# A split first exp, a moved half quarter, a moved exp and a warm-up of short matmuls in a fused convolution and feed-forward kernel

## The chip, the cores and the metric

The kernel runs on one NeuronCore of a Trainium2 chip. The metric is the device time of one execution in microseconds. TensorE (PE in the profile) multiplies, VectorE (DVE) and ScalarE (ACT) do elementwise work, GpSimd (POOL) makes masks and issues some of the DMAs, SyncE (SP) issues the others. "PEld" is TensorE loading weights, which it can do while it multiplies.

## The reference

A dynamic convolution over the last seven rows, with weights from a softmax, and behind it a feed-forward layer with a squared relu:

```python
w = weight_gen - np.max(weight_gen, axis=-1, keepdims=True)      # (8, 4096, 8 heads, 7 taps)
w = np.exp(w)
w = w / (np.sum(w, axis=-1, keepdims=True) + 1e-09)
x_pad = np.concatenate([np.zeros((B, 6, D)), x], axis=1)          # x: (8, 4096, 192)
x_unf = x_pad[:, np.arange(S)[:, None] + np.arange(7)[None, :], :].reshape(B, S, 7, 8, 24)
y = np.einsum('bshk,bskhg->bshg', w, x_unf).reshape(32768, 192)
h = np.maximum(y @ w_in, 0.0)                                     # w_in: (192, 2048)
out = h * h @ w_out                                               # w_out: (2048, 192)
```

## The kernel before

**Blocks.** The 32768 tokens go through in blocks: `BLOCKS` has two of 512 tokens and then 31 of 1024. Blocks are numbered from 0 in the code; the text calls block 0 "block one". For each block:

- *Softmax.* A `Softmax` object holds 8, 16 or 32 rows of tokens per partition (`FIRST = 8` for the first ones, which cover 1024 tokens) and 6 rows of overlap. `load` fetches `weight_gen`, `exp(lo, hi)` runs on ScalarE (L238), `total` sums on VectorE (L245), `recip` takes reciprocals (L252) and `scale` multiplies into `v_first` or `v_big` (L260), by four operations for each 8 rows.
- *Rows and bands.* The scaled weights are brought to one row of tokens per partition (`wr`), by DMAs through `move_rows` and `wr_load`, and for the first block by TensorE: `select_rows` multiplies with a selection matrix `sel` (L372), eight matmuls for each of five tiles, and `copy_rows` copies from PSUM (L381). `st_band` then spreads `wr` with a mask into a band matrix `bd` on VectorE (L395).
- *Convolution.* `st_conv` multiplies `x` with the bands on TensorE (L455, L527, L493), and copies the result to `y`, in the blocks that matter here on ScalarE (L467, L538).
- *Units.* `st_unit` computes one unit of the hidden layer into a PSUM tile `h` of two banks, from a ring of three that the convolution shares. In the first two blocks `first_unit` does it (L557) with two full-array matmuls ("both") and a pair of half-array matmuls that run side by side ("upper"); even units do "both" first and "upper" last, odd units the other way round. In all later blocks a unit is six half-array matmuls (L572). A relu on ScalarE (L586) follows, and a square on VectorE (L590) into `g`. The first two blocks have 8 units, the others 16.
- *Second matmul.* `quarters` is a generator; each step of it, a half quarter, is `st_mm2` (L621) over half of the hidden layer for 256 tokens, 16 full-array matmuls in the first two blocks, 32 half-array ones afterwards. It accumulates in the PSUM tiles `o0` and `o1`. Every second step for a quarter ends in `o_sum`: a copy on ScalarE (L635) and, in the later blocks, a sum on VectorE (L637), then for every second quarter a store. The steps lag behind the units.

**Order.** The order is written out by hand. `plans` gives one string for each of the first four blocks: `u` is a unit, `M` the next half quarter, `C` the next block's convolution, `E3` the next piece of exp of softmax part 3, `S3` its sums, reciprocal and scale, `B4` the bands of sub-block 4, `L5` a load of part 5 on SyncE, `P` the selection of the last rows of block two. Later blocks follow a steady string. Each engine works in program order.

**The start.** Before the first real work TensorE runs `spin(21)`: 21 matmuls of 512 columns on a zeroed tile `warm` into `wp`, which shares a PSUM bank with `o0` (L687). Meanwhile the first weights and `x` arrive, and ScalarE and VectorE do the first softmax: `s0.exp`, `s0.total`, `s0.recip`, `s0.scale`. Then come `select_rows(0, ...)`, the copies, the bands, and `st_conv_first(0, ...)`.

Of the kernel before, what the change touches and what calls it, by code (L numbers as in the profile page):

```python
# [9 lines left out]
def kernel(  # L10
# [26 lines left out]
    nc = tc.nc  # L37
# [13 lines left out]
    P = 128  # L51
# [47 lines left out]
    FIRST = 8  # L99
# [8 lines left out]
    def row_select():  # L108

        nc.gpsimd.affine_select(  # L110
            out=sel, in_=sel, pattern=[[-1, NSEL]], compare_op=AluOp.not_equal,
            fill=1.0, base=FIRST - 1, channel_multiplier=FIRST,
        )
# [543 lines left out]
    with nc.allow_low_precision("fp16 matmul pipeline"), tc.manual_schedule():  # L657
# [18 lines left out]
        warm = const.tile([P, TB], f16, name="warm")  # L676
# [3 lines left out]
        for v in v_first:  # L680
            nc.vector.memset(v, 0.0)

        wp = ps_o.tile([P, TB], f32, name="wp", tag="o0")

        def spin(n):
            for i in range(n):
                nc.tensor.matmul(out=wp, lhsT=warm[:, 0:P], rhs=warm, start=True, stop=True)  # L687

        s0, s1, s2 = parts[:3]
        spin(21)  # L690
        row_select()
        band_mask()
        s0.load(nc.sync)
# [3 lines left out]
        load_w_in(w_i[:, 1, 0], 1, nc.gpsimd)  # L697
        x_load(1)
        s1.load(nc.gpsimd)
        s0.exp(0, s0.rh)  # L700
        s0.total(0, s0.rh)
        s0.recip(0, s0.rh)
        s0.scale(0, s0.rh, nc.vector)
        x_cast(0, nc.scalar.copy, 0, 1)
# [24 lines left out]
        for q in range(4):  # L729
# [9 lines left out]
        steady_spread = "MuMuuu" * 2 + "MuCMuuu" + "MuMuuu"  # L739
        plans = {  # L740
            0: "u P B1 u u u E1 C S1 u u M u u",
            1: "L3 u u B2 M E2 B3 u M E2 u u S2 S2 u M u C u M",
            2: "L4 u u u E3 M u u u M B4 u u u u M B5 S3 u u u u M u C E3 u",
            3: "L5 L6 u u u M S3 u u u M u M E4 u u B6 u M u M B7 u u u E4 M u M C S4 u",
        }


# [49 lines left out]
        for j in range(len(plans), NBLK):  # L797
            plan, u = [], 0
# [59 lines left out]
        for j in range(NBLK):  # L858
# [5 lines left out]
            u = 0  # L864
# [76 lines left out]
```

The softmax here doesn't subtract the row's maximum and nothing guards it: scores larger than these inputs give would overflow.

## Time and profile before

| | us |
|---|---|
| median of 4 runs | 731.7 |
| lowest, highest | 731.32, 732.82 |
| profiled execution | 731.76 |
| its span, first to last instruction | 730.1 |
| TensorE busy in the span | 724.9 (99%) |
| VectorE, ScalarE busy | 626.7 (86%), 612.2 (84%) |

Rows of the timeline read: start in us, duration in us, engine, line, operation, output and input tiles with shapes, count; in brackets the idle time of the engine just before and what ended it. Rows of one kind that follow closely are merged, the duration then reaching from the first start to the last end. A matmul's end is modelled, so the distance between starts says more than a duration. Rows of the chain read: start, duration, engine, tile, line, count.

### The profile page before, as it was taken

The page shows a single profiled execution, that of the slowest core. Times are in us where ns is not written, and L with a number is a line of the kernel's source. Part 1 is how long each engine was busy: PE and PEld are TensorE (multiplying, and loading weights), DVE is VectorE, ACT ScalarE, POOL GpSimd, SP SyncE. Part 2 cuts the span into 40 slices and gives each one's busy share as a digit, 9 for nine tenths or more (in the row PEclk, how much of TensorE's full clock was granted, in tenths as well). Part 3 has the DMA queues.
Part 4 walks back from the last instruction along what each step waited for, and adds up shares of the span by engine and source line. Part 5 has one row for each costly group of instructions (what it writes and reads, how often), then busy time and mean ns, then how long its engine had stood idle before and what let it go on. Part 6 is the DMA issues. An engine that isn't in the chain of part 4 may idle for free.

```text
span 730.1 us, 30988 instructions
## 1 busy us (share of the span) xinstructions
PE 724.9 (99%) x14053; PEld 531.2 (73%) x14053; DVE 626.7 (86%) x836; ACT 612.2 (84%) x733; POOL 99.8 (14%) x145
## 2 busy tenths in 40 slices
PE   9999999999999999999999999999999999999998
PEld 4657888777777777777777777777777777777777
DVE  7998998998898988888988888988889988778753
ACT  5999888888888888888888888888888888888883
POOL 8131223321001100011000010010000110001000
PEclk9999999999999999999999999999999999999999
DMA  9555455685345442455442554343544325444012
GB/s 208 112 106 114 82 102 99 132 149 130 86 66 137 90 92 59 82 117 124 76 67 58 136 104 88 56 79 114 107 84 86 57 52 118 66 87 78 30 45 68
DMA packets 125984, 68.30 MB, mean 94 GB/s; under 512 B 85321, under 2 KB 122140, under 8 KB 125340
## 3 DMA queue, kind: packets, MB, share of 16 engines
q0 software_dynamic: 46192, 19.43, 22.6%
q1 hardware_dynamic: 79516, 46.79, 22.3%
q8 instruction: 110, 1.80, 1.0%
q14 instruction: 22, 0.18, 0.1%
q10 hardware_dynamic: 144, 0.10, 0.0%
HBM read 50.18 MB, written 28.70 MB: 108 GB/s over the span
## 4 chain that ended last, share of the span: by engine, by line
PE 99%; ACT 1%; issue 0%; DVE 0%
PE o L621 47%; PE h L572 44%; PE yp L493 4%; PE h L557 2%; PE yp L527 1%; PE wp L687 1%; PE yp L455 0%; ACT y L538 0%; PE pr L372 0%; ACT t L586 0%; ACT wr L381 0%; ACT w_i L721 0%; ACT y L467 0%; ACT xt L336 0%; ACT o_sb L635 0%
## 5 line engine op out<-in xcount | busy, mean ns | idle before, releaser
L586 ACT ACTIVATE t<-h 128x1024 f16<-128x1024 f32 x512 | 496.4, 1026 | 60.6 <-PE h L572 59.1
L621 PEld LDWEIGHTS <-g 64*128 64x128 f16 (+1 forms) x8032 | 345.2, 94 | 54.3 <-issue 2.5
L621 PE MATMUL o<-w_o,g 64*128 64x192 f16 (+1 forms) x8032 | 380.7, 243 | 0.2 <-issue 0.2
L590 DVE TENSOR_TENSOR g<-t 128x2048 f16<-128x2048 f16 (+1 forms) x287 | 307.3, 1105 | 30.0 <-ACT t L586 29.9
L572 PE MATMUL h<-y,w_p 64*128 64x512 f16 x2400 | 291.8, 376 | 0.0
L572 PEld LDWEIGHTS <-w_p 64*128 64x128 f16 x2400 | 114.1, 94 | 94.6
L395 DVE TENSOR_TENSOR bd<-wr,mask 128x4160 f16<-128x4160 f16 (+4 forms) x90 | 149.6, 1686 | 1.1 <-ACT wr L381 0.8
L637 DVE TENSOR_TENSOR o_sb<-o,o_sb 128x384 f32<-128x384 f32 x123 | 68.4, 556 | 61.2 <-ACT o_sb L635 60.3
L321 POOL DMA_DIRECT2D xt<-in_x_dram x63 | 52.7, 839 | 415.6 <-PE yp L493 362.5
L635 ACT COPY o_sb<-o 128x384 f32<-128x384 f32 x129 | 61.6, 477 | 45.7 <-PE o L621 45.2
L572 PE MATMUL h<-y,w_i 64*128 64x512 f16 x576 | 71.0, 377 | 0.3 <-ACT t L586 0.3
L572 PEld LDWEIGHTS <-w_i 64*128 64x128 f16 x576 | 32.6, 94 | 20.3 <-issue 1.6
L493 PEld LDWEIGHTS <-xt 128*32 128x32 f16 x2000 | 24.6, 95 | 10.6 <-issue 10.6
L260 DVE TENSOR_TENSOR v_big<-ex,rcp 128x112 f16<-128x112 f32 (+5 forms) x180 | 29.8, 236 | 2.0 <-DMA vd<-v_big 1.0
L503 DVE CAST y<-yp 128x1024 f16<-128x1024 f32 x25 | 30.4, 1218 | 0.0
L493 PE MATMUL yp<-bd,xt 128*32 128x104 f16 (+1 forms) x2000 | 28.4, 210 | 0.0
L238 ACT ACTIVATE ex<-wg 128x560 f32<-128x560 f32 (+4 forms) x38 | 25.9, 682 | 1.7 <-DMA wg<-in_weight_gen_dram 1.7
L245 DVE TENSOR_REDUCE ssum<-ex 128x80 f32<-128x560 f32 (+4 forms) x38 | 25.3, 666 | 1.2 <-ACT ex L238 1.2
L503 ACT CAST y<-yp 128x1024 f16<-128x1024 f32 x25 | 25.2, 1007 | 0.0
L252 DVE RECIPROCAL rcp<-ssum 128x80 f32<-128x80 f32 (+4 forms) x38 | 22.8, 600 | 1.3
L311 POOL DMA_DIRECT2D xt<-in_x_dram x7 | 3.9, 555 | 120.8 <-PE yp L493 109.4
L355 POOL DMA_DIRECT2D wr<-v_first x24 | 13.0, 562 | 24.8 <-DVE v_first L260 13.7
(41 smaller groups left out, 116.1 us busy)
## 6 DMA issues: line engine op xcount, KB each, us to landing
out_dram<-o_sb SPq DMA_DIRECT2D x63, 384.0 KB
xt<-in_x_dram POOLq DMA_DIRECT2D x42, 240.0 KB, 4.8
wg<-in_weight_gen_dram SPq DMA_DIRECT2D x4, 1064.0 KB
xt<-in_x_dram POOLq DMA_DIRECT2D x21, 192.0 KB, 4.8
wr<-vd SPq DMA_DIRECT2D x38, 80.0 KB
vd<-v_big SPq DMA_DIRECT2D x5, 512.0 KB
y<-y SPq DMA_DIRECT2D x100, 24.0 KB
wg<-in_weight_gen_dram SPq DMA_DIRECT2D x3, 616.0 KB
```

What stands on the lines that cost most here:

```text
L238: nc.scalar.activation(out=self.ex[:, lo:hi].rearrange("p r g k e -> p (r g) k e"), in_=self.wg[:, lo:hi].rearrange("p r (g e) k -> p (r g ...
L260: eng.tensor_tensor(out=bass.AP(tensor=v.tensor, offset=v.offset + lo * H * SL + lo % SL * 2 + g * SL * 2, ap=[list(v.ap[0]), [H * SL + 2, ...
L321: eng.dma_start(out=dst[:, first:last], in_=ap)
L395: nc.vector.tensor_tensor(out=bd_t[j][:, H * lo : H * (lo + len(tiles) * n)].rearrange("p (g m c) -> p g m c", g=shape[1], c=2 * SL), in0= ...
L493: nc.tensor.matmul(out=yp[p0 : p0 + 32, k - k0, a:b], lhsT=x_t[s][:, i, c0 : c0 + 32], rhs=bd[:, head // 2, e, 0 : b - a], start=True, sto ...
L503: copy(out=y[:, k0 : k0 + 2], in_=yp)
L572: nc.tensor.matmul(out=h[:, half], lhsT=w_in_chunk(w, u, slot, half), rhs=y_t[j][r0 : r0 + RT, k], start=(slot == 0), stop=(slot == NK - 1 ...
L586: nc.scalar.activation(out=t1[:, e], in_=h, func=ActF.Relu)
L590: nc.vector.tensor_tensor(out=g[:, a : e + 1], in0=t1[:, a : e + 1], in1=t1[:, a : e + 1], op=AluOp.mult)
L621: nc.tensor.matmul(out=oo[:, cc * Dm : (cc + 1) * Dm], lhsT=g[r0 : r0 + n, cc * P : (cc + 1) * P], rhs=w_o[r0 : r0 + n, fc, :], start=(fc ...
L635: nc.scalar.copy(out=o_sb, in_=o[0][:, c])
L637: nc.vector.tensor_tensor(out=o_sb, in0=o[1][:, c], in1=o_sb, op=AluOp.add)
```

## The change

Three edits in the program's order of work, none in what is computed.

- The warm-up runs 46 matmuls of 196 columns instead of 21 of 512.
- The first softmax's exp and sums run in two pieces, rows 0 to 7 and rows 8 to 13; reciprocal and scale stay whole.
- In block two (`plans[1]`) the second `M` stands behind one more unit. In block three (`plans[2]`) the second piece of `E3` leaves the end of the plan, and stands in block four (`plans[3]`) behind two units.

```diff
+        WARM = 196
         wp = ps_o.tile([P, TB], f32, name="wp", tag="o0")
 
         def spin(n):
             for i in range(n):
-                nc.tensor.matmul(out=wp, lhsT=warm[:, 0:P], rhs=warm, start=True, stop=True)
+                nc.tensor.matmul(
+                    out=wp[:, 0:WARM], lhsT=warm[:, 0:P], rhs=warm[:, 0:WARM],
+                    start=True, stop=True,
+                )
 
         s0, s1, s2 = parts[:3]
-        spin(21)
+        spin(46)
...
-        s0.exp(0, s0.rh)
-        s0.total(0, s0.rh)
+        for lo, hi in ((0, FIRST), (FIRST, s0.rh)):
+            s0.exp(lo, hi)
+            s0.total(lo, hi)
         s0.recip(0, s0.rh)
...
-            1: "L3 u u B2 M E2 B3 u M E2 u u S2 S2 u M u C u M",
-            2: "L4 u u u E3 M u u u M B4 u u u u M B5 S3 u u u u M u C E3 u",
-            3: "L5 L6 u u u M S3 u u u M u M E4 u u B6 u M u M B7 u u u E4 M u M C S4 u",
+            1: "L3 u u B2 M E2 B3 u u M E2 u S2 S2 u M u C u M",
+            2: "L4 u u u E3 M u u u M B4 u u u u M B5 S3 u u u u M u C u",
+            3: "L5 L6 u u E3 u M S3 u u u M u M E4 u u B6 u M u M B7 u u u E4 M u M C S4 u",
```

## The prediction

> **What bounds the kernel now.** I read the page first: shares of busy time, then the chain that ended last.
>
> ```profile
> span 730.1 us, 30988 instructions
> PE 724.9 (99%) x14053; PEld 531.2 (73%) x14053; DVE 626.7 (86%) x836; ACT 612.2 (84%) x733; POOL 99.8 (14%) x145
> PE 99%; ACT 1%; issue 0%; DVE 0%
> ```
>
> TensorE is the chain almost from end to end, so time is won only where it waits or works badly. The change touches the first 60 us; a microsecond that TensorE gains there reaches the end only if no other engine takes over behind it. The second view is the timeline of the first 12 us.
>
> ```profile
> 1.26 7.14 PE L687 MATMUL wp<-warm 128*128 128x512 f16 x21 [1.26 <-DVE warm L678]
> ...
> 3.84 0.94 ACT L238 ACTIVATE ex<-wg 128x784 f32<-128x784 f32 x1 [1.75 <-DMA wg<-in_weight_gen_dram]
> ...
> 4.81 0.97 DVE L245 TENSOR_REDUCE ssum<-ex 128x112 f32<-128x784 f32 x1 [1.17 <-ACT ex L238]
> ...
> 5.81 0.85 DVE L252 RECIPROCAL rcp<-ssum 128x112 f32<-128x112 f32 x1
> ...
> 6.30 1.61 PEld L687 LDWEIGHTS <-warm 128*128 128x128 f16 x8 [0.21 <-issue]
> 6.70 1.46 DVE L260 TENSOR_TENSOR v_first<-ex,rcp 128x112 f16<-128x112 f32 x8
> ...
> 8.24 1.33 PE L372 MATMUL pr<-v_first,sel 128*128 128x64 f16 x40
> ```
>
> Two things end at nearly one time. The softmax (exp, sums, reciprocal, scale) is done at 6.70 + 1.46 = 8.16. The warm-up matmuls are issued 0.427 us apart until about 6.25 (their weight loads stand at 5.51, 5.93, then 6.30) and 0.215 apart afterwards: TensorE's rate doubles there. (The granted clock reads 1.00 throughout; it does not show this step, the spacing does.) The last one's columns end at 8.24, and there the row selection starts. The third view is the chain in order of time.
>
> ```profile
> 23.26 1.32 PE o L621 x16
> 24.58 0.75 PE h L557 x4
> 25.34 1.43 PE o L621 x16
> 26.76 2.37 PE h L557 x12
> ...
> 51.74 1.50 ACT y L538 x2
> 53.24 0.31 issue
> 53.54 1.03 ACT t L586
> 54.58 0.04 issue
> 54.62 0.82 PE h L572 x6
> ```
>
> The second matmul's sixteen (L621) cost 1.32 in one place, 1.43 in another. From 51.74 to 54.62 the chain leaves TensorE for ScalarE: two copies of `y`, a piece of exp (the 0.31 of "issue": the exp stands at 53.13), then a relu.
>
> **Part 1, the start: exp and sums in two pieces, short warm-up.** ScalarE: the exp of 784 holds the engine 0.84 (the next cast starts at 4.68). Later rows have the two sizes: 448 takes 0.62 and the next starts 0.52 after, 336 takes 0.52 and holds 0.41. So the pieces end at 3.84 + 0.62 = 4.46 and 4.36 + 0.52 = 4.88, against 4.78: 0.09 of extra ScalarE time, ahead of a cast whose successor waits for its DMA until 6.18 anyway. VectorE: the sums take 0.61 (64 wide) and 0.50 (48 wide); the first starts at 4.49, the second behind it at about 5.02 and ends at 5.52, against 5.78. Reciprocal and scale are unchanged, so they end 0.26 earlier: scale at 7.90, seen by TensorE at about 7.94 (0.05 for the hand-over, as from the memset's end at 1.21 to 1.26).
>
> Warm-up: 0.427 / 512 columns is 0.834 ns each, so 196 columns take 0.163 before the step. A weight load takes 0.15 there and fits behind the matmul before it, just. After the step, sixteen L621 matmuls of 192 columns, each with its own load of 128, take 1.32, 0.0825 each; 196 columns 0.084. By 6.25 (6.25 - 1.26) / 0.163 = 30.5 are through, the other 15.5 take 1.30: the end is at 7.55 instead of 8.24. If the loads did not hide, each would cost 0.31 and 0.18 and the end would be near 11.8. The first bound is taken, for the L621 rows stream at their column count with the same loads.
>
> TensorE's own order says that the first two selection matmuls need the first half of the scale, the third its last operation. The third now starts at 8.24 + 2 x 0.03 = 8.30; it will at 7.94. Gain 0.36. It takes both edits: the split alone leaves the warm-up end at 8.24, the short warm-up alone leaves the scale at 8.16 + 0.05 = 8.21 (gain 0.09). What follows is a chain of small copies on ScalarE (8.67 to 12.6) that moves as one. Its other inputs must be there: `x_st` landed by 6.18, the mask is done at 6.27, GpSimd reads `w_st` at 9.82 and ScalarE only at 11.23, the first `w_o` loads are issued from 10.08 with 5.4 to 6.3 to landing and needed at 18.77. Nothing is late, so 0.36; from nothing (an input I take for landed is not) to 0.36.
>
> The Trainium skill (TensorE: Matmul & The Clock Gate, "Back-to-back issue gap") speaks against short matmuls: it gives about 81 ns for a stream of 128-column matmuls with loads, where the columns alone would take 56. An estimate by that, 25 ns more for each of the last 15.5, ends the warm-up at 7.93 and changes nothing.
>
> **Part 2, block two: the half quarter goes behind one more unit.** An even unit of `first_unit` ends on the pair of half-array matmuls, an odd one on the full-array pair. A unit is three streams of 0.2157 (0.647) plus one change between the two kinds: 0.75 says 0.10 for a change. The half quarter after odd unit 1 costs 1.32, the one after even unit 2 costs 1.43, and the three units behind it 2.37 = 3 x 0.647 + 4 x 0.107, the fourth change being the one on return. Moved behind unit 3 both changes at its edges go: 2 x 0.107 = 0.21. It issues 16 matmuls and one ScalarE copy of `o` (0.48), no store. The copy and the second exp piece now stand behind unit 3's relu instead of ahead of it; the bank is wanted again 8 us later, that exp's sum only at 34.03. The cover that could fail is VectorE: the last band for the next convolution ends at 30.92, the convolution starts at 31.13 and needs that band some 0.2 later. Arriving 0.21 earlier uses that up and no more: 0 to 0.06 lost, I take 0.
>
> **Part 3, blocks three and four: the exp goes behind two units.** ScalarE holds 0.41 for it at 53.13. Without it the relu of the last unit starts at 53.13 and ends at 54.15, and the third unit of block four, which waits for that relu's bank, starts at 54.21 instead of 54.62. But ScalarE has the same work until the copy of `o`:
>
> ```profile
> 57.16 0.53 ACT L635 COPY o_sb<-o 128x384 f32<-128x384 f32 x1
> ...
> 57.72 0.56 DVE L637 TENSOR_TENSOR o_sb<-o,o_sb 128x384 f32<-128x384 f32 x1
> ...
> 58.52 1.50 PE L621 MATMUL o<-w_o,g 64*128 64x192 f16 x32
> ```
>
> With the exp ahead of the third relu, copy and sum still end at 57.69 and 58.28, and the next half quarter, which writes the same two banks, cannot start before about 58.33. So 0.41 is won at 54.6 and 58.52 - 58.33 = 0.19 stays. Bounds: nothing, and the whole loss there, 3.15 from 52.11 to 55.26 for four units of 0.647, 0.56. On SyncE the load of a later weight block, which reuses that exp's input, now waits until about 56.3 (issued at 53.68 before). Queued behind it are row loads that need VectorE's scale of 59.9 anyway, and the weights are not used before block five: free.
>
> **The sum.** 0.36 + 0.21 + 0.19 = 0.76. The profiled execution took 731.76 (span 730.1 and 1.66 around it), the median is 731.7: 731.76 - 0.76 = **731.0**. Nothing after 62 us is touched, and the chain there is TensorE without a wait over 0.22.
>
> **Rivals.**
> *Larger gain.* The step of the rate stands at 6.25 in one execution; nothing fixes it there. For each microsecond that it comes later the old warm-up ends 0.5 later, the new one too, but with 0.39 to spare: up to about 0.4 more. With the whole 0.56 of part 3 that is 0.36 + 0.4 + 0.21 + 0.56 = 1.53: 730.2. For it: the runs before reach 732.82. Against: the profiled run is not faster than the median.
> *The start does not move,* because an input lands later than I read (`w_st` at 11.23 is the candidate), and part 3 is swallowed: 0.21 alone, 731.5.
> *Slower: the rate falls back.* The warm-up ends 0.69 sooner, a gap of up to 0.39 opens, and then come 4.4 us of thin selection and convolution work. If TensorE's rate halved there, it would need what it needed at first, 4.99 us of dense work, to rise, and lose half of it: 731.0 + 2.5 = 733.5. It decides where the first units after 12.3 show 0.43 instead of 0.216 between full matmuls. Against: the same thin stretch was survived before.
>
> The same page (Part 1, "What's actually happening") has the clock raised after one busy window of about 3.4 us that runs free of the kernel's start. By that the step would come between 4.7 and 8.1 and the mean gain of part 1 would be some 0.1 more, 730.9; one trace cannot show it.
>
> **How the numbers follow.** The sum 0.50, the larger gain 0.24, the start that does not move 0.18, the fall-back 0.08. About 0.2% (1.46 us) is what a measurement of this kernel can tell from no change: faster means under 730.24, slower over 733.16. The larger gain lies about that line, and most of it counts as faster: 0.22 with a little of the sum's tail; the fall-back gives slower 0.07; the rest is 0.71. Range 730.1 to 731.9: down to the larger gain, up past the second rival by the spread of the runs; the fall-back and the tails stay out.
>
> **What would show it.** Warm-up matmuls 0.163 then 0.084 apart, the last ending near 7.55; two sums at 4.49 and 5.02, the scale ending near 7.9, the selection's third matmul at 7.94. In block two 1.32 for each half quarter and units without the 0.11 beside them. The third unit of block four 0.41 nearer to its convolution, the half quarter after it held by the sum on VectorE. I am wrong if the first units of block one do not start 0.36 earlier (12.3 instead of 12.65), or if the gain at 62 us is not the gain at the end.

## The result and the profile after

The changed kernel takes 730.95 us (median of 41 runs, 730.36 to 731.73), the kernel before 731.83 (59 runs, 731.28 to 732.82). The ratio is 0.9987, 95% interval 0.9983 to 0.9992: 0.13% faster, inside the 0.2% that the prediction called no change. The forecast was 731.0.

The page of the changed kernel, the same three lines as before:

```profile
span 729.1 us, 31040 instructions
PE 723.2 (99%) x14078; PEld 531.3 (73%) x14078; DVE 626.6 (86%) x837; ACT 612.3 (84%) x734; POOL 100.2 (14%) x145
PE 98%; ACT 0%; DVE 0%; DMA 0%; issue 0%
```

The span is 1.0 shorter. TensorE fell from 99% to 98% of the chain, and ScalarE from 1% to 0%: the start is no longer a run of warm-up matmuls, and the detour over ScalarE in block four is gone. The start in the timeline:

```profile
1.26 5.43 PE L688 MATMUL wp<-warm 128*128 128x196 f16 x46 [1.26 <-DVE warm L678]
...
3.94 1.02 ACT L238 ACTIVATE ex<-wg 128x448 f32<-128x448 f32 x2 [1.85 <-DMA wg<-in_weight_gen_dram]
4.59 1.03 DVE L245 TENSOR_REDUCE ssum<-ex 128x64 f32<-128x448 f32 x2 [0.95 <-ACT ex L238]
...
6.54 1.46 DVE L260 TENSOR_TENSOR v_first<-ex,rcp 128x112 f16<-128x112 f32 x8
...
7.43 0.22 PE L372 MATMUL pr<-v_first,sel 128*128 128x64 f16 x2 [0.74 <-DVE v_first L260]
...
8.06 1.27 PE L372 MATMUL pr<-v_first,sel 128*128 128x64 f16 x38 [0.41 <-DVE v_first L260]
...
12.39 0.91 PE L557 MATMUL h<-y,w_i 128*128 128x512 f16 x4
```

The warm-up is over by 6.7. Two selection matmuls run at 7.43 on the first half of the scale, and the third waits until 8.06 for its last operation: VectorE decides the start now. The first unit of block one starts at 12.39 instead of 12.65. The chain in order of time, blocks two and four:

```profile
23.02 1.32 PE o L621 x16
24.34 1.51 PE h L557 x8
25.84 1.32 PE o L621 x16
27.17 1.51 PE h L557 x8
28.67 1.32 PE o L621 x16
...
51.69 2.88 PE h L572 x24
54.58 1.32 PE o L621 x32
55.90 1.94 PE h L572 x18
57.84 1.50 PE o L621 x32
```

All half quarters of block two cost 1.32 now. ScalarE is gone from the chain at 51.7, but one half quarter costs 1.50 where 1.32 is normal. Why stands in the timeline:

```profile
55.38 0.55 ACT L238 ACTIVATE ex<-wg 128x336 f32<-128x336 f32 x1
...
55.79 1.06 ACT L586 ACTIVATE t<-h 128x1024 f16<-128x1024 f32 x1
...
56.69 0.53 ACT L635 COPY o_sb<-o 128x384 f32<-128x384 f32 x1
...
57.25 0.56 DVE L637 TENSOR_TENSOR o_sb<-o,o_sb 128x384 f32<-128x384 f32 x1 [0.46 <-ACT o_sb L635]
...
57.87 1.25 PEld L621 LDWEIGHTS <-g 64*128 64x128 f16 x30 [0.31 <-issue]
```

Exp, relu, copy and sum stand in a row; the sum ends at 57.81, and the half quarter, of which two loads and the first matmul (57.66) had gone ahead, goes on at 57.87.

### The profile page after: what moved, and what is told of

Its sections match the earlier page's. It is cut to its first block, busy times and chain, and to the rows that moved or that the text cites. A ratio compares the mean times of both kernels' runs of the same rounds, so it can differ in the third digit from the quotient of the medians.

```text
span 729.1 us, 31040 instructions
## 1 busy us (share of the span) xinstructions
PE 723.2 (99%) x14078; PEld 531.3 (73%) x14078; DVE 626.6 (86%) x837; ACT 612.3 (84%) x734; POOL 100.2 (14%) x145
## 4 chain that ended last, share of the span: by engine, by line
PE 98%; ACT 0%; DVE 0%; DMA 0%; issue 0%
PE o L621 47%; PE h L572 44%; PE yp L493 4%; PE h L557 2%; PE yp L527 1%; DMA wg<-in_weight_gen_dram 0%; PE yp L455 0%; DVE v_first L260 0%; PE pr L372 0%; DVE ssum L245 0%; DVE rcp L252 0%; ACT wr L381 0%; ACT w_i L726 0%; ACT ex L238 0%; ACT y L467 0%
## 5 line engine op out<-in xcount | busy, mean ns | idle before, releaser
L637 DVE TENSOR_TENSOR o_sb<-o,o_sb 128x384 f32<-128x384 f32 x123 | 68.4, 556 | 61.0 <-ACT o_sb L635 60.1
L572 PEld LDWEIGHTS <-w_i 64*128 64x128 f16 x576 | 30.9, 94 | 21.3 <-issue 1.2
L260 DVE TENSOR_TENSOR v_big<-ex,rcp 128x112 f16<-128x112 f32 (+5 forms) x180 | 29.8, 236 | 2.5 <-DMA vd<-v_big 1.5
L238 ACT ACTIVATE ex<-wg 128x448 f32<-128x448 f32 (+4 forms) x39 | 26.0, 670 | 1.8 <-DMA wg<-in_weight_gen_dram 1.8
L245 DVE TENSOR_REDUCE ssum<-ex 128x64 f32<-128x448 f32 (+4 forms) x39 | 25.3, 652 | 1.0 <-ACT ex L238 1.0
```

What stands on the lines that cost most here:

```text
L238: nc.scalar.activation(out=self.ex[:, lo:hi].rearrange("p r g k e -> p (r g) k e"), in_=self.wg[:, lo:hi].rearrange("p r (g e) k -> p (r g ...
L260: eng.tensor_tensor(out=bass.AP(tensor=v.tensor, offset=v.offset + lo * H * SL + lo % SL * 2 + g * SL * 2, ap=[list(v.ap[0]), [H * SL + 2, ...
L572: nc.tensor.matmul(out=h[:, half], lhsT=w_in_chunk(w, u, slot, half), rhs=y_t[j][r0 : r0 + RT, k], start=(slot == 0), stop=(slot == NK - 1 ...
L637: nc.vector.tensor_tensor(out=o_sb, in0=o[1][:, c], in1=o_sb, op=AluOp.add)
```

## The experiments

The theory: three local gains that add up, each with one condition. The start gains only when neither the warm-up nor the scale ends late; the half quarter gains by the changes between full-array and half-array matmuls; the exp gains until ScalarE and VectorE hold the next half quarter. The rivals: the warm-up alone decides the start; ScalarE's order decides in block two; the whole 0.41 stays in block four. Most verdicts rest on distances between starts in the traces. They repeat to about 0.03, while a comparison of eleven runs leaves some 0.6 us open on each side.

| us in the trace | exp starts | scale ends | first unit | first unit to conv. of block 3 | conv. of block 4 to first unit behind the held half quarter |
|---|---|---|---|---|---|
| before | 3.84 | 8.16 | 12.65 | 18.48 | 9.26 |
| changed | 3.94 | 8.00 | 12.39 | 18.29 | 9.01 |
| e1, short warm-up | 3.99 | 8.30 | 12.70 | 18.49 | 9.26 |
| e2, split | 4.02 | 8.08 | 12.70 | 18.48 | 9.27 |
| e3, half quarter | 3.99 | 8.31 | 12.71 | 18.27 | 9.27 |
| e4, exp moved | 4.01 | 8.33 | 12.73 | 18.50 | 9.00 |
| e5, both at the start | 4.03 | 8.10 | 12.50 | 18.50 | 9.26 |
| e6, exp behind M | 4.06 | 8.13 | 12.53 | 18.28 | 8.86 |
| e7, 23 matmuls | 3.95 | 8.02 | 13.90 | 18.29 | 9.00 |
| e8, pairs exchanged | 4.05 | 8.37 | 12.95 | 18.71 | 9.27 |
| e9, changed again | 3.95 | 8.01 | 12.41 | 18.28 | 9.00 |
| e10, as e6 again | 3.97 | 8.04 | 12.44 | 18.27 | 8.86 |
| e11, 34 matmuls | 3.93 | 7.99 | 12.39 | 18.28 | 9.01 |

### Each edit alone (e1 to e4), and both at the start (e5)

e1 holds the first hunk of the diff, e2 the second, e3 and e4 one plan each:

```diff
-        spin(21)                        # e1: 46 matmuls of 196 columns
+        spin(46)
-        s0.exp(0, s0.rh)                # e2
+        for lo, hi in ((0, FIRST), (FIRST, s0.rh)):
...
-            1: "L3 u u B2 M E2 B3 u M E2 u u S2 S2 u M u C u M",      # e3
+            1: "L3 u u B2 M E2 B3 u u M E2 u S2 S2 u M u C u M",
-            3: "L5 L6 u u u M S3 ...                                  # e4, and E3 out of plan 2
+            3: "L5 L6 u u E3 u M S3 ...
```

> The kernel before with the 46 short warm-up matmuls alone; exp and sums stay whole. Theory A (two ends at one time, both needed): the warm-up ends early, the scale still ends at about 8.16, the selection's third matmul starts at about 8.21 and the first unit of block one at about 12.56 instead of 12.65, a gain of 0.09. Averaged over executions in which the step of TensorE's rate comes late, the old warm-up would lose more, so the time may be up to 0.4 lower. Rival R1 (the warm-up's end alone decides the start): first unit at about 12.39 as in the changed kernel, gain 0.26 or more.

> The kernel before with exp and sums in two pieces alone, 21 long warm-up matmuls. Theory A: the scale ends at about 7.9 to 8.0, but the selection starts where the long warm-up ends: 8.24 if the step of the rate comes at 6.25, 7.2 to 7.5 if it comes at 4.2 as in the trace of the changed kernel (then the scale decides and the gain is 0.24). Times between 0 and 0.25 lower. R1: no gain at all, whatever the step.

> The kernel before with both edits at the start, the plans as before. Theory A: the first unit of block one at 12.3 to 12.4, 0.26 to 0.36 earlier than before, which is more than the two edits alone give together wherever the step of the rate comes at 6.25 or later; from there on the distances are those of the kernel before (18.48 to the convolution of block three). R1: the same as the short warm-up alone.

Measured, against the kernel before with its interval: e1 731.78 (ratio 0.9996, 0.9987 to 1.0004), e2 731.83 (0.9997, 0.9988 to 1.0006), e5 731.57 (0.9992, 0.9984 to 1.0001). The times separate nothing; the traces do. From exp's start to the scale's end it is 4.31 to 4.32 with whole pieces and 4.06 to 4.07 with split ones, in every trace: the split is worth 0.25 on VectorE. But e2 does not get it, as its own rows show:

```profile
1.26 7.19 PE L687 MATMUL wp<-warm 128*128 128x512 f16 x21 [1.26 <-DVE warm L678]
8.29 0.89 PE L372 MATMUL pr<-v_first,sel 128*128 128x64 f16 x25
```

Its scale is ready at 8.08 and the selection starts at 8.29, straight behind the long warm-up. e1 is early with its warm-up and waits for the scale at 8.30. Both have the first unit at 12.70; e5, with both, at 12.50. R1, for which e1 should have had the whole gain, falls. Not as I expected: e1's first unit is no 0.09 earlier, because exp started 0.15 later there than in the profile of before. Counted from exp's start, which takes out when `wg` landed, the first unit comes after 8.81 before, 8.71 in e1, 8.68 in e2, and 8.45 to 8.47 in the six traces with both edits and at least 34 warm-up matmuls. By this count e1 gains 0.10, e2 0.13, and both together 0.34 to 0.36.

There is a second reading. In the traces of e3 and e4, whose start is that of the kernel before, the long warm-up was *not* late; this is e3's row of weight loads:

```profile
3.80 0.15 PEld L687 LDWEIGHTS <-warm 128*128 128x128 f16 x1 [0.28 <-issue]
4.17 2.69 PEld L687 LDWEIGHTS <-warm 128*128 128x128 f16 x13 [0.22 <-issue]
```

TensorE's rate doubles at about 4.15, not 6.25, and the 21 matmuls end by 7.4, a microsecond before the scale. Counted from exp, the first unit comes after 8.72 in e3 and e4, as early as with the short warm-up in e1, so there a short warm-up has nothing to gain. That the split alone would gain its 0.25 in such an execution follows from these rows, but no run shows it: in e2 the step came at 6.35. Which edit does the work depends on where the step falls in that execution; the pair gains either way.

> The kernel before with the half quarter of block two moved alone. Theory A (changes between full-array and half-array matmuls cost 0.107 each, two go): the two half quarters after units 1 and 3 cost 1.32 each, the pairs of units between them 1.51, and from the first unit of block one to the convolution of block three it is 0.21 less (18.48 before, so 18.27). Rival R2 (ScalarE's order is what gains): the half quarter still costs 1.43 and the gain shows as an idle time that is gone. Time 0.2 lower.

18.27, as expected to the hundredth, with every half quarter of block two at 1.32. Time 731.42 (0.9994, 0.9985 to 1.0002).

> The kernel before with the exp piece moved behind two units of block four alone. Theory A: from the start of block four's convolution (50.58) to the third unit 0.41 less, but the second half quarter of that block is held by the sum on VectorE; from that convolution to the first unit behind the held half quarter (59.84 before) 9.02 instead of 9.26, a gain of 0.24. Rival R3 (the whole 0.41 stays): 8.85. Time 0.2 to 0.25 lower for A, 0.4 for R3.

9.00 against 9.02 expected; R3 falls. The half quarter costs 1.50 here too. Time 731.89 (0.9999, 0.9991 to 1.0008), which shows nothing at 0.25.

### What makes a half quarter cost 1.43 (e8)

```diff
-        pairs = (upper, both) if u % 2 else (both, upper)
+        pairs = (both, upper) if u % 2 else (upper, both)
```

> The kernel before with the order of the two kinds of matmul in first_unit exchanged: even units now do the half-array pair first and end on the full-array matmuls, odd units end on the half-array pair. Plans as before. Theory A (0.107 for each change of kind): the half quarter behind unit 2 of block two now costs 1.32, those behind odd units (blocks one and two) 1.43, with 0.11 more in the units behind them, so that from the first unit of block one to the convolution of block three it is 0.1 to 0.4 more than 18.48. R2 (ScalarE's order): the half quarters cost what they cost before.

The chain of e8, block two:

```profile
23.58 1.43 PE o L621 x16
25.01 0.86 PE h L557 x4
25.87 1.32 PE o L621 x16
27.19 2.26 PE h L557 x12
29.45 1.43 PE o L621 x16
```

The picture is inverted: behind even unit 2 the half quarter costs 1.32 and its neighbours, which cost 1.32 before, now 1.43. ScalarE's order is untouched, so R2 falls: it is the change between full-array and half-array matmuls. The stretch is 18.71, 0.23 more. The time of e8 is a single execution, the profiled one, of 732.84; nothing is read from it. (The first unit is also 0.25 to 0.3 later, because it now begins with the part of `y` that VectorE copies last.)

### What holds the half quarter in block four (e6, e10)

```diff
-            3: "L5 L6 u u E3 u M S3 ...
+            3: "L5 L6 u u u M E3 S3 ...
```

> The changed kernel, but in block four the exp piece stands behind the first half quarter, so that the copy of o goes ahead of it on ScalarE. Theory A (the second half quarter is held by copy and sum, which the exp delays): copy and sum end 0.4 earlier, the second half quarter costs 1.32 instead of 1.50, and from block four's convolution to the first unit behind it 8.84 instead of 9.01. VectorE's sums of that piece wait a little longer for the exp. Time 0.1 to 0.2 lower than the changed kernel. Rival R4 (the half quarter is held by something else, say the g of the last unit): still 1.50 and 9.01, no gain.

> The kernel with the exp piece behind the half quarter once more, timed on the same chip as the changed kernel. Theory A: 0.15 lower than the changed kernel (8.86 against 9.01 in the trace), which is less than the comparison can resolve; both faster than before.

The timeline of e6, ScalarE and VectorE:

```profile
56.43 0.54 ACT L635 COPY o_sb<-o 128x384 f32<-128x384 f32 x1
56.79 0.58 ACT L238 ACTIVATE ex<-wg 128x336 f32<-128x336 f32 x1
57.00 0.56 DVE L637 TENSOR_TENSOR o_sb<-o,o_sb 128x384 f32<-128x384 f32 x1
...
57.80 1.50 PE L621 MATMUL o<-w_o,g 64*128 64x192 f16 x32
```

The sum ends at 57.56, before the half quarter starts, which now costs 1.32 in the chain, and the stretch is 8.86, 0.15 less than with the change. e10 repeats it: 8.86. R4 falls. In time, e10 took 730.42 (0.9981 of before, 0.9973 to 0.999) beside 730.57 for the changed kernel on the same chip (e9: 0.9984, 0.9975 to 0.9992), and e6 730.54 (0.9982, 0.9973 to 0.9991). It beats the kernel before; that it beats the changed kernel is shown in the trace only, 0.15 is below what the times resolve.

### How much warm-up it needs (e7, e11)

`spin(46)` becomes `spin(23)` in e7, `spin(34)` in e11.

> The changed kernel with 23 warm-up matmuls of 196 columns instead of 46, which end at about 5.0. It tries how much of the warm-up the rate needs. If TensorE keeps or reaches its full rate without it: first unit at 12.39 and no change of time. If the rate is not up or falls back in the gap from 5.0 to 7.4 and the thin stretch behind it (the prediction's slower rival): full matmuls of the first units 0.43 apart, up to 5 us long, and 1 to 2.5 more in time.

> The changed kernel with 34 short warm-up matmuls, between the 23 that left the rate low until about 12 and the 46. At half rate they last until 1.26 + 34 x 0.163 = 6.8, and the step has come between 4.2 and 6.3 in every profile with a warm-up of that length or more. Theory A6 (the rate rises when dense work lasts until the step): the step comes, the first unit of block one at about 12.4 to 12.5, time as the changed kernel. Rival R6 (the warm-up must reach to within a fraction of a microsecond of the selection): the rate falls back in the gap from 5.5 or so to 7.5, first unit 0.5 to 1.5 later.

e7 took 732.49 (1.0005, 0.9996 to 1.0014), about 1.5 more than the changed kernel. Its chain at the start:

```profile
8.07 2.19 PE pr L372 x38
10.25 0.47 PE yp L455 x15
10.72 0.54 PE pr L372 x8
11.26 0.47 PE yp L455 x13
11.73 0.55 PE pr L372 x8
```

Eight selection matmuls take 0.54 where the changed kernel has 0.34. The 23 matmuls end at about 5.0, still at half rate, and the rate stays down through the gap and the thin stretch until about 12.9, where groups of four convolution matmuls go from 0.087 apart to 0.044: the prediction's slower rival, real, but not at 46. The first unit starts at 13.90, 1.5 late, and the distances behind it are those of the changed kernel, so no full matmul paid any more. This is one trace; as the step has come as early as 4.15, another execution of e7 may reach it before its warm-up ends, and its ten times spread from 731.72 to 733.19. e11 gets its step before its 34 matmuls end (by 6.2) and keeps the rate through more than a microsecond of gap: first unit at 12.39, time 731.01 (0.9988, 0.9979 to 0.9997). R6 falls.

### The part that nobody changed (e9)

> The changed kernel once more, for two questions. First, the part of its profile after 72 us was 0.29 shorter than that of the kernel before, though nothing is changed there; in the runs so far that part lies anywhere from 654.5 to 655.3 whatever the kernel. Theory A: that is chance, so this second profile of the same kernel may differ from the first by up to 0.8 there, while its stretches before 62 us repeat to 0.02 (18.28 from first unit to convolution of block three, 9.01 from block four's convolution to the first unit behind the held half quarter). Rival R5 (the change shortens the later part): 654.5 to 654.6 again. Second, it is timed beside the next kernel. Time 0.8 to 0.9 below the kernel before.

Before, 72 us to the last copy took 654.87, with the change 654.58, and again 654.48. The last figure is what R5 (the change shortens the later part) had forecast, so e9 alone does not decide against R5. The time of e9, 730.57, is 1.28 under the kernel before, where I had expected 0.8 to 0.9; the interval leaves room for both. All kernels lie between 654.28 (e11) and 655.34 (e2). Block by block, the spread sits in two places, between about 94 and 140 us, where a block takes 22.53 or 22.54 when undisturbed and up to 23.24; all other blocks agree within 0.06. The first of them in the chain of the kernel before:

```profile
97.36 1.07 PE o L621 x25
98.43 0.22 issue
98.65 0.50 PE o L621 x7
```

and in the chain of e4:

```profile
97.20 1.07 PE o L621 x25
98.27 0.47 issue
98.74 0.50 PE o L621 x7
```

TensorE stops in the middle of a half quarter, for a reason that the trace does not name, by a different amount in each execution. A store of `out` keeps the DMA engines busy at that moment, but the same store runs beside a half quarter without a stop in the changed kernel, so it does not explain the stop by itself. The second place, from about 117 us on, has a cause in the traces: VectorE's scale there (L260) waits for the DMA that stores the tile `v_big` to `vd`, the sum on VectorE (L637) behind it comes late, and a half quarter that needs the sum's bank is held. The block grows with that wait: 22.53 to 22.56 with waits up to 1.12 (0.99 before), 22.82 with 1.46 (changed), 22.95 with 1.58 (e8), 23.11 to 23.21 with 1.74 to 1.85 (e5, e7, e2). So 0.29 of the profile's 1.0 is no term of my sum. That it is all chance is not settled: the kernels with the whole change, in one form or another, lie at 654.28 to 654.90 (mean 654.59), the others at 654.48 to 655.34 (mean 654.95), and the ranges overlap.

## Why the prediction held

**The sum.** 0.76 was forecast; to the first unit behind the held half quarter the profile gains 59.84 - 59.12 = 0.72, the medians 0.88 (731.83 - 730.95), and the interval of the ratio allows 0.6 to 1.2. That 731.0 lies within 0.05 of the median is partly luck: one term was 0.10 too large, another 0.06 too small, and the span has 0.29 that belongs to no term. Both signs by which the prediction was to be called wrong came up: the first units start 0.26 earlier and not 0.36, and the gain at 62 us, 0.72, is not the 1.0 at the end of the profile. The mechanisms of the three parts held; the size of the start did not.

**The start, 0.36.** The profile shows 0.26. Exp to scale shrank by the 0.26 that was worked out, the hand-over of 0.05 and the third matmul's wait are there. As a gain from profile to profile the term was too large by 0.10, because the sum was made from one execution in which `wg` landed early (exp at 3.84; 3.93 to 4.06 in all others): the scale was ready earlier there than usual, so the warm-up held it up. Counted from exp's start the gain is the 0.36 of the sum (8.81 to 8.45). The warm-up's end, 7.55 expected, was 6.7, because the step came at about 4.15; the spacing is 0.163 before the step, in e7 too, and 0.084 behind it, so the 25 ns more for each short matmul that the prediction weighed did not appear.

**The half quarter, 0.21.** 0.19 in the profile, 0.21 in e3. The cover I doubted, the last band, was never used up: I had left VectorE's end at 30.92, but its four band operations take 4.66 instead of 4.86 and end at 30.47, and the convolution starts at 30.68 behind the unit before it, without a wait.

**The exp, 0.19.** 0.25. The mechanism is the predicted one. Copy and sum end 7.11 and 7.70 after block four's convolution starts, as worked out. The size is off by 0.06 because two loads and the first matmul of the held half quarter had already gone when the sum released the rest; I had it start as a whole. SyncE's load went out at 55.96, behind the exp, and nobody waited.

**The rivals.** The larger gain needed the whole 0.56 in block four; 0.25 stayed, and no profile with a long warm-up shows a step later than 6.35. The start that does not move did not happen: `w_st` was there. The fall-back was not seen with 46 or 34 matmuls; at 23 it cost 1.5, where I had priced 2.5, because the rate was up again just before the dense work began.

## What to carry to other kernels

Where two chains end together, cost them as a pair: shortening either alone can show nothing, and which one is last can change from run to run. When TensorE alternates between full-array and row-tiled matmuls, order the work so that equal kinds meet; each change cost 0.107 here, and the reorder that saved two of them added no instruction. Before moving work on an engine that is briefly the bound, follow its queue to the next thing that it releases: the exp moved ahead of a copy gave back 0.15 of the 0.41 it had won.

## What the runs showed of the hardware

The step in TensorE's rate is not at a fixed place. In the long warm-ups the spacing changed at about 4.15 (e3), 4.6 (e4), 6.25 (before, e8) and 6.35 (e2), with the first matmul at 1.26 in all. The granted clock read 1.00 through all of it. The Trainium skill (TensorE: Matmul & The Clock Gate, "What's actually happening") explains such a spread by a busy window of about 3.4 us that runs free of the kernel, and gives it as 500 ns either way. A spread there is, but it is 2.2 us here, and e3's step came 2.9 us after the first matmul, less than the window; the measurement decides.

The half-rate state costs little where TensorE is mostly waiting: e7 ran nearly the whole first selection and convolution in it, and lost 1.5.

The price of changing the kind of matmul, 0.107 each time, I had taken from three rows of one trace, and it held when the order was inverted. The Trainium skill (TensorEngine Tiling (Array Packing), "Key Properties") says that changing the tiling mode drains TensorE. The traces show a price at each change, which the page leaves out; they do not show what it consists of.
